# A new hand-written order of all operations in a gated recurrence with a highway layer

## The chip, the cores and the metric

The kernel runs on one core of one Trainium2 chip. The metric is the device time of one execution in microseconds (us). The kernel before took 206.16 us (median of three runs, 205.93 to 207.3).

A core has five engines that work side by side, each through its own queue in order: TensorE (PE; its weight loads are listed as PEld), VectorE (DVE), ScalarE (ACT), GpSimd (POOL), and SyncE (SP), which here only issues transfers. Engines wait for each other by semaphores. TensorE writes to PSUM; GpSimd works on SBUF alone.

## The reference

A recurrence along the sequence with a forget gate, and then a highway layer on each token:

```python
# x, f_logit: (4, 6336, 256) float32; lower_bound: (256,)
sig = 1.0 / (1.0 + np.exp(-f_logit))
f = lower_bound + (1.0 - lower_bound) * sig
h = 0
for t in range(S):
    h = f[:, t] * h + (1.0 - f[:, t]) * x[:, t]
    y[:, t] = h
# on y as (25344, 256), with w_h, w_t (256, 256) and b_t (256,)
H = np.maximum(y @ w_h, 0.0)
T = 1.0 / (1.0 + np.exp(-(y @ w_t + b_t)))
out = T * H + (1.0 - T) * y
```

## The kernel before

The 25344 tokens are cut into 29 units of 2, 4 or 8 blocks of 128 tokens (`parts`: units 0 and 1 have 2 blocks, 2 to 4 have 4, 5 to 26 have 8, 27 has 4, 28 has 2). Features lie in two halves of 128, numbered 0 and 1. Each unit goes through the same steps. A step is a token in a long string, `order`: a letter, the unit, a dot, the half (or piece), and after a colon the number of the buffer it takes. A trailing `v` puts a step on VectorE that otherwise goes to ScalarE (f, c) or GpSimd (b, e).

- l, x (line 256, SP): load the logits and x of a unit, 1 MB each for 8 blocks.
- u (268, ScalarE): u = sigmoid(-logits), so that 1 - f = (1 - lower_bound) * u.
- b (276, GpSimd or VectorE): bv = u * x for one half; two inputs in SBUF.
- i (284, TensorE): transposes u into PSUM (uT). f (295 ScalarE, 293 VectorE): f = 1 + ncc * uT, ncc being lower_bound - 1.
- p (304, TensorE): transposes bv into PSUM (bT).
- s (323, VectorE): the scan y = f * y + bT along the tokens; it carries over from unit to unit.
- z, g (335 and, with the weights already loaded, 115; TensorE): the two products of y with the weights.
- t (348, ScalarE): t = sigmoid(z + b_t). d (352, VectorE): d = max(ncc * y, g), that is H - y (y itself is kept without its factor 1 - lower_bound).
- e (358, GpSimd or VectorE): d = d * t, in pieces; two inputs in SBUF. A unit of 8 blocks has both halves in one tile of 2048 columns, cut at 1024 and 1536 into e.0, e.1 and e.2; units 9 to 21 have one piece of 2048. Smaller units have one piece for each half.
- o (380, 381, TensorE): transposes y (times 1 - lower_bound) and d back and adds them in PSUM. c (393 ScalarE, 391 VectorE): copies that to SBUF. w (397, SP): stores it, 512 KB at a time for most units.

Tokens without a number are the set-up: pc and pb transpose lower_bound and b_t, cc computes ncc and cc from lower_bound (lines 200 and 201, VectorE), cb copies the bias, dg scales the identity (217, VectorE), IW and WHa/WTa prepare the weights (212 GpSimd, 228 ScalarE). A k token gives TensorE idle matmuls to do.

The program issues the steps exactly in the order of the string, and each engine keeps that order (`tc.keep_in_program_order`). So the string is each engine's queue, and a step that waits holds up everything behind it on its engine.

One function ties GpSimd to VectorE beyond the data:

```python
def shared(ins, gpsimd):
    if not gpsimd:
        held[:] = [ins]
    elif held:
        tc.add_manual_dep(ins.ins, held.pop().ins.name, ..., reason="shared port")
```

It is called for each b and e, for IW and for dg: a product of GpSimd waits for the last product of VectorE that stands ahead of it in the string. Nothing makes a product of VectorE wait for GpSimd's earlier one.

Of the kernel before, what the change touches and what calls it, by code (L numbers as in the profile page):

```python
# [57 lines left out]
b6.0:5 f6.1:2 d4.0 k*3:1 p6.1:0 s6.1:4 i6.0:1 l8:2 u7:3 z5.1:1 g5.1:2 x8:2 b7.1:6 b7.0:7 f6.0:0 t4.0 t5.1:2 i7.1:1 p6.0:0
z5.0:0 f7.1:1 d5.1:2 t5.0 o3.0:1 g5.0:2 i7.0:1 c3.0:3 s6.0:5 e5.1v w1.0 l9:3 e4.0 x9:3 w0.0 e5.2v p7.1:0 l10:4 w2.0 d5.0 e5.0
g6.0:0 z6.1:1 z6.0:2 u8:0 f7.0:3 t6.1:1 i8.0:1 e4.1v b8.0:1 b8.1:0 s7.1:6 f8.0v:2 l11:5 w3.0 t6.0 x10:4 x11:5 u9:1 d6.0:0  # L60
i8.1:0 g6.1:1 p7.0:1 s7.0:7 o5.1:2 f8.1:0 c5.1:1 o5.0:0 i9.1:0 d6.1 e6.0 p8.1:1 c5.0:0 f9.1:1 e6.2 z7.0:2 t7.0:0 o4.0:0
p8.0:0 c4.0:2 u10:2 w5.1 b9.1:3 e6.1 l12:0 w4.0 l13:1 g7.1:1 s8.1:2 i9.0:1 g7.0:2 o6.0:0 s8.0:3 i10.1:0 f9.0:3 b9.0:2 x12:0
# [375 lines left out]
```

## Time and profile before

| | before |
|---|---|
| time, median of 3 runs | 206.16 us (205.93 to 207.3) |
| profiled execution: span, first to last instruction | 204.7 us; its own time is not given, the median lies 1.46 us above the span |
| busy: TensorE, VectorE, ScalarE, GpSimd | 191.6, 193.0, 193.1, 175.6 us |
| granted TensorE clock | 0.996 |
| DMA | 78.4 MB on one queue, 94.7% of 16 engines' span |

The profile is of one execution. A row of a group gives line, engine, operation, `out<-in`, shapes and count, then the busy time in us and the mean ns of one instruction, then the engine's idle time just before them and what ended it. A row in order of time gives start (us), duration (us), engine, line, operation and, in brackets, the idle time before. A row of a wait gives who waited for whom, the sum in us, how often, and the longest. Consecutive instructions of an engine overlap a little in their records, so a busy time is less than the sum of durations.

### The profile page before, as it was taken

The page shows a single profiled execution, that of the slowest core. Times are in us where ns is not written, and L with a number is a line of the kernel's source. Part 1 is how long each engine was busy: PE and PEld are TensorE (multiplying, and loading weights), DVE is VectorE, ACT ScalarE, POOL GpSimd, SP SyncE. Part 2 cuts the span into 40 slices and gives each one's busy share as a digit, 9 for nine tenths or more (in the row PEclk, how much of TensorE's full clock was granted, in tenths as well). Part 3 has the DMA queues.
Part 4 walks back from the last instruction along what each step waited for, and adds up shares of the span by engine and source line. Part 5 has one row for each costly group of instructions (what it writes and reads, how often), then busy time and mean ns, then how long its engine had stood idle before and what let it go on. Part 6 is the DMA issues. An engine that isn't in the chain of part 4 may idle for free. (4 is left out here: it accounts for less than half of the span.)

```text
span 204.7 us, 4658 instructions
## 1 busy us (share of the span) xinstructions
PE 191.6 (94%) x1826; PEld 131.9 (64%) x1826; DVE 193.0 (94%) x162; ACT 193.1 (94%) x201; POOL 175.6 (86%) x98
## 2 busy tenths in 40 slices
PE   7889999989899899999999999999998999999990
PEld 2455656576567757757666577776776677677680
DVE  2799999999999999999999999999999999999990
ACT  4799999999999999999999999999999999999771
POOL 3146699899996999799999979999979999989960
PEclk9999999999999999999999999999999999999998
DMA  5999999999999999999999999999999998970986
GB/s 176 387 415 429 410 421 415 413 424 420 422 419 411 429 423 415 425 415 422 428 402 426 429 417 419 418 425 423 413 337 400 425 390 307 352 283 22 396 330 241
DMA packets 16413, 78.68 MB, mean 384 GB/s; under 512 B 1796, under 2 KB 2568, under 8 KB 10760
## 3 DMA queue, kind: packets, MB, share of 16 engines
q1 hardware_dynamic: 16384, 78.39, 94.7%
q8 instruction: 14, 0.23, 0.4%
q14 instruction: 7, 0.06, 0.1%
q10 hardware_dynamic: 8, 0.00, 0.0%
HBM read 52.43 MB, written 25.95 MB: 383 GB/s over the span
## 5 line engine op out<-in xcount | busy, mean ns | idle before, releaser
L276 POOL TENSOR_TENSOR bv<-u,x 128x1024 bf16<-128x1024 f16 (+2 forms) x53 | 104.2, 1988 | 14.8 <-DVE d L358 5.7
L323 DVE TENSOR_TENSOR_SCAN y<-f,y,bT 128x1024 bf16<-128x1024 f16 (+5 forms) x56 | 106.9, 1925 | 0.2
L358 POOL TENSOR_TENSOR d<-d,t 128x512 bf16<-128x512 bf16 (+3 forms) x32 | 70.4, 2213 | 4.1 <-DVE d L358 1.8
L352 DVE SCALAR_TENSOR_TENSOR d<-y,ncc,g 128x1024 bf16<-128x1024 bf16 (+2 forms) x58 | 63.2, 1105 | 0.3 <-PE g L115 0.2
L348 ACT ACTIVATE t<-z,bt 128x1024 bf16<-128x1024 f32 (+2 forms) x58 | 62.4, 1112 | 0.8 <-PE z L115 0.8
L295 ACT ACTIVATE f<-uT,ncc 128x1024 f16<-128x1024 f16 (+2 forms) x55 | 60.8, 1120 | 0.8 <-DVE y L323 0.2
L393 ACT COPY o<-op 128x1024 f32<-128x1024 f32 (+2 forms) x53 | 52.8, 1036 | 1.9 <-ACT t L348 1.0
L268 ACT ACTIVATE u<-l 128x2048 f16<-128x2048 f32 (+2 forms) x29 | 51.5, 1776 | 2.5 <-DMA l<-in_f_logit_dram 2.5
L380 PE MATMUL op<-diag,y 128*128 128x128 f16 x396 | 49.7, 219 | 0.9 <-ACT t L348 0.4
L381 PE MATMUL op<-ident_b,d 128*128 128x128 bf16 x396 | 49.7, 219 | 0.8 <-POOL d L358 0.8
L381 PEld LDWEIGHTS <-d 128*128 128x128 bf16 x396 | 44.0, 113 | 4.8 <-POOL d L358 1.7
L380 PEld LDWEIGHTS <-y 128*128 128x128 bf16 x396 | 44.2, 113 | 2.3
L335 PE MATMUL z<-y,w_sb 128*128 128x512 bf16 (+1 forms) x116 | 40.0, 368 | 0.8 <-DVE d L352 0.3
L335 PE MATMUL g<-y,w_sb 128*128 128x512 bf16 (+1 forms) x116 | 40.3, 368 | 0.0
L304 PE MATMUL bT<-ident_f,bv 128*128 128x128 f32 x198 | 32.1, 278 | 2.9 <-DVE y L323 1.1
L115 PE MATMUL g<-y,w_sb 128*128 128x512 bf16 x88 | 33.3, 379 | 0.0
L115 PE MATMUL z<-y,w_sb 128*128 128x512 bf16 x88 | 33.3, 379 | 0.0
L284 PE MATMUL uT<-ident_h,u 128*128 128x128 f16 x396 | 31.4, 219 | 2.0 <-DVE y L323 1.1
L284 PEld LDWEIGHTS <-u 128*128 128x128 f16 x396 | 25.9, 98 | 11.1 <-issue 3.1
L335 PEld LDWEIGHTS <-w_sb 128*128 128x128 f16 x232 | 22.3, 98 | 15.7 <-ACT f L295 0.2
L304 PEld LDWEIGHTS bT<-ident_f,bv 128*128 128x128 f32 x198 | 22.1, 140 | 13.3 <-issue 4.7
L115 PEld LDWEIGHTS <-w_sb 128*128 128x128 f16 x176 | 17.2, 98 | 15.8 <-issue 1.7
(35 smaller groups left out, 53.6 us busy)
## 6 DMA issues: line engine op xcount, KB each, us to landing
out_dram<-o SPq DMA_DIRECT2D x48, 512.0 KB, 9.7
l<-in_f_logit_dram SPq DMA_DIRECT2D x22, 1024.0 KB, 14.0
x<-in_x_dram SPq DMA_DIRECT2D x22, 1024.0 KB, 14.3
l<-in_f_logit_dram SPq DMA_DIRECT2D x4, 512.0 KB, 6.3
x<-in_x_dram SPq DMA_DIRECT2D x4, 512.0 KB, 7.6
x<-in_x_dram SPq DMA_DIRECT2D x3, 256.0 KB, 3.7
l<-in_f_logit_dram SPq DMA_DIRECT2D x3, 256.0 KB, 4.3
out_dram<-o SPq DMA_DIRECT2D x2, 256.0 KB, 14.8
```

What stands on the lines that cost most here:

```text
L115: return pe.add_instruction(mybir.InstMatmult(name=nc.get_next_instruction_name(), start_tensor_calc=start, stop_tensor_calc=stop, tile_si ...
L276: shared(pin(e.tensor_mul(bv[:, :nb // 2].rearrange("p k d j -> p k j d"), st[n]["u"][:, :nb, own].rearrange("p (k j) d -> p k j d", j=2), ...
L284: pin(nc.tensor.transpose(uT[:, j * P:(j + 1) * P], st[n]["u"][:, j, h * P:(h + 1) * P], ident_h))
L295: pin(nc.scalar.activation(to, of, AF.Identity, scale=ncc[:, h:h + 1], bias=1.0))
L304: pin(nc.tensor.transpose(words[:, k:k + g * (P - 1) + 1:g], pair, ident_f))
L323: pin(nc.vector.tensor_tensor_scan(y[:, c:e], st[n]["f", h][:, c:e], st[n]["bT", h][:, c:e], 0.0 if fresh else carry[h], op0=ALU.mult, op1 ...
L335: pin(nc.tensor.matmul(p[:, a:e], w, half(n, "y", ki)[:, a:e], start=ki == 0, stop=ki == NH - 1))
L348: pin(nc.scalar.activation(half(n, "t", m), st[n]["z", m][:, :tokens(n)], AF.Sigmoid, bias=bt[:, m:m + 1]))
L352: pin(nc.vector.scalar_tensor_tensor(half(n, "d", m), half(n, "y", m), ncc[:, m:m + 1], st[n]["g", m][:, :tokens(n)], op0=ALU.mult, op1=AL ...
L358: shared(pin(e.tensor_mul(st[n]["d"][:, a:c], st[n]["d"][:, a:c], st[n]["t"][:, a:c])), not eng)
L380: pin(nc.tensor.matmul(o, half(n, "y", h)[:, cols], diag[:, h], start=True, stop=False))
L381: pin(nc.tensor.matmul(o, half(n, "d", h)[:, cols], ident_b, start=False, stop=True))
```

## The change

Only the string changes. It has 850 tokens in both versions, and they name the same computation; their places, some buffers, and some of the trailing `v` differ:

- f on VectorE: units 1.0, 8.0, 10.0; now also 28.0.
- e on VectorE: before 0.0, 0.1, 1.0, 1.1, 2.0, 2.1, 3.1, 4.1, 5.1, 5.2, 7.1, 7.2, 8.1, 11.0, 15.0, 16.0, 19.0, 23.0, 23.2, 24.2, 26.1, 26.2 (22 pieces). After: 0.0, 0.1, 1.0, 1.1, 4.1, 6.1, 7.1, 8.2, 11.0, 15.0, 16.0, 19.0, 23.0, 23.2, 25.0, 25.1, 26.2, 27.1, 28.0, 28.1 (20 pieces). The others are GpSimd's.
- c on VectorE: before 11.0, 26.1, 26.2, 27.1; after 1.0, 11.0, 26.0.
- The five b on VectorE stay (0.0, 0.1, 1.0, 1.1, 2.1).
- Buffers for o: numbers 0 to 3 for nearly all units before, 0 to 4 after.

The beginning, the places around e15, e16 and e19, and the end, of the diff:

```diff
-k*3:a0 x0:0 pc:0 l0:0 l1:1 cc u0:0 k*3:1 pb:2 i0.0:1 k*4:0 dg wh u1:1 b0.1v:0 f0.0:0 b0.0v:1 i1.0:0 x1:1 l2:2 wt IW f1.0v:1 p0.0:1
-WHa cb i0.1:0 s0.0:0 f0.1:2 x2:2 b1.1v:2 b1.0v:3 k*2:0 i1.1:1 k*1:0 p0.1:0 f1.1:3 p1.0:1 s0.1:1 k*1:0 p1.1:0 l3:3 g0.0:0
-s1.0:2 g0.1:1 u2:2 s1.1:3 x3:3 k*1:2 i2.1:1 d0.1:0 l4:4 WTa d0.0 g1.0:2 i2.0:0 g1.1:1 z1.1:0 b2.1v:4 f2.1:0 d1.1:1 d1.0
...
-c14.0:0 f19.1:2 z17.1:1 p18.0:0 e16.0v c14.1:1 b19.1:6 w14.0 b19.0:7 x21:3 e15.0v i19.0:1 t17.1:2 g17.0:2 z17.0:0 f19.0:3
...
-e28.1 w26.1 c27.1v:3 o28.0:2 c27.0 o28.1:a1 w26.0 c28.0:2 c28.1:4 w27.0 w28.0 w28.1
+x0:0 k*1:0 l0:0 k*3:a0 u0:0 i0.0:1 pc:1 cc i0.1:0 b0.0v:0 k*3:2 f0.1:0 l1:1 f0.0:1 p0.0:0 wh u1:1 pb:0 b0.1v:1 p0.1:1 k*4:1 s0.0:0 x1:1
+s0.1:1 IW i1.1:0 f1.1:2 i1.0:1 l2:2 WHa b1.1v:2 k*2:2 b1.0v:3 p1.1:0 wt f1.0v:3 x2:2 p1.0:1 cb u2:2 g0.0:1 k*3:2 g0.1:0 s1.1:2 s1.0:3
+dg l3:3 i2.1:0 WTa f2.1:1 x3:3 i2.0:1 z1.0:2 d0.1:0 b2.1v:4 z0.0:0 l4:4 p2.1:0 f2.0:0 t1.0:0 d0.0 u3:3 s2.1:4 z1.1:1 b2.0:5 t0.0:1
...
+s17.1:1 o14.0:2 f18.1:2 w11.1 t16.0:2 t16.1 i19.0:0 x20:2 f19.0:1 o14.1:0 b19.0:5 b18.0:4 z17.0:1 c14.1:0 c14.0:1 t17.0:0 e16.0v e15.0v
+b18.1:1 p18.0:1 i19.1:0 o16.1:0 b20.1:0 g17.0:2 c16.1:2 f19.1:0 s18.0:4 o16.0:1 p18.1:1 z17.1:0 w13.0 d17.0:1 c16.0:4 g17.1:2 s18.1:5
...
+w23.0 b28.1:6 o25.0:0 z26.1:1 o25.1:a1 c25.0:0 g26.1:0 d26.0:1 s27.0:3 e25.2 e26.0 t26.1 o25.2:2 o25.3:1 d26.1 c25.1 p28.0:0 w24.1
+c25.2:4 e26.2v c25.3 s28.0:6 g27.0:a1 z27.0:2 t27.0:2 o26.3:0 w24.0 w22.1 c26.3:1 e26.1 d27.0:2 z27.1:1 w20.1 t27.1 p28.1:0 o26.2:2
+g27.1:a1 o26.1:0 o26.0:1 c26.2 s28.1:7 e27.0 z28.0:a0 d27.1 w25.0 z28.1:a1 g28.1:2 e27.1v w25.1 c26.1:3 t28.0:1 o27.0:0 c26.0v o27.1:a0
+g28.0:1 d28.1:0 t28.1 e28.1v d28.0 c27.0:2 e28.0v o28.0:2 c27.1 o28.1:0 w26.1 c28.0:0 w26.0 w27.0 w28.0 c28.1:4 w28.1
```

More of the change, by code (lines that the diff above doesn't have):

```diff
@@ L58 @@
[L58 to L62, printed above, removed]
@@ new lines @@
+o21.1:1 g23.1:2 f28.1:0 e22.0 i28.0:0 b25.0:2 o22.0:0 c21.1:3 f28.0v:1 u26:0 d23.1 g24.1:1 p25.0:1 s25.0:0 i25.1:0 z24.1:2 c22.0:1
+x26:2 x27:3 e22.2 b25.1:3 w21.1 l27:4 z24.0:0 f25.1:3 b26.1:1 t24.1:2 i26.1:0 x28:4 w22.0 d24.1:2 p25.1:1 z23.0:2 t24.0 w20.0 f26.1:2
+e24.2 b26.0:4 g24.0:1 s25.1:1 t23.0 o22.1:0 u27:3 p26.1:0 z25.1:2 c22.1:3 d24.0 e24.0 e23.1 b27.0:5 e24.1 w21.0 i26.0:1 b27.1:7 e23.2v
+e23.0v t25.1:1 f26.0:3 g25.0:1 o23.1:0 z25.0:2 p26.0:1 s26.1:4 c23.1:1 i27.1:0 d25.0:0 o23.0:0 w23.1 s26.0:5 t25.0 o24.1:1 f27.1:2
```

71 lines of the change are left out of this document (32 added, 39 removed).

## The prediction

> **What bounds the kernel now.** I read the page's busy shares first, then the engines' busy time by stage, then the groups of instructions with their shapes, then the waits, and last the order of time at the start, at the end and around VectorE's products. The page:
>
> ```profile
> span 204.7 us, 4658 instructions
> PE 191.6 (94%) x1826; PEld 131.9 (64%) x1826; DVE 193.0 (94%) x162; ACT 193.1 (94%) x201; POOL 175.6 (86%) x98
> ```
>
> Three engines at 94% say little, because the share mixes the ramp, the middle and the tail. So I cut the span where GpSimd's first bv begins (12.37), where its first e begins (26.70), where its last bv begins (189.06) and where its last e ends (199.62):
>
> ```profile
> core 0: us, PE busy (x) PEld busy (x) DVE busy (x) ACT busy (x) POOL busy (x), PEclk, DMA share, GB/s
> 0.00:12.37 12.37, 10.31 (x50) 4.39 (x50) 6.87 (x19) 8.09 (x15) 2.49 (x13) 1.00 0.82 305
> 12.37:26.70 14.33, 13.34 (x113) 8.45 (x113) 14.09 (x20) 14.12 (x20) 10.01 (x7) 1.00 1.02 421
> 26.70:189.06 162.36, 157.18 (x1545) 111.18 (x1546) 162.13 (x111) 161.98 (x153) 154.45 (x71) 1.00 0.97 393
> 189.06:199.62 10.56, 10.31 (x115) 7.64 (x112) 9.92 (x14) 7.96 (x14) 8.63 (x9) 1.00 0.91 358
> 199.62:204.70 5.08, 0.45 (x5) 0.28 (x5) 0.00 (x0) 0.90 (x3) 0.00 (x1) 0.83 0.63 241
> ```
>
> In the middle VectorE (DVE) idles 0.23 of 162.36 us and ScalarE (ACT) 0.38. No reordering can squeeze those two there; only less work on them can. GpSimd (POOL) idles 7.91 there, and in the tail 10.56 - 8.63 = 1.93, together 9.84. ScalarE has room in the tail, 10.56 - 7.96 = 2.60, and in the first stage. The waits say what the idle time is:
>
> ```profile
> POOL bv L276 <- DVE d L358: 5.7, 5, 1.4
> DVE ncc L200 <- PE lbT L194: 3.0, 1, 3.0
> ACT u L268 <- DMA l<-in_f_logit_dram: 2.5, 2, 1.3
> DVE f L293 <- PE uT L284: 1.4, 1, 1.4
> ```
>
> GpSimd's largest wait is for VectorE's e (the manual dependency in `shared`). ScalarE waited for loads only at the start, though the DMA engines are 97% busy in the middle: loads arrive in time, without much to spare.
>
> **The change, part by part.** The terms come from these groups (busy us, mean ns):
>
> ```profile
> L358 DVE TENSOR_TENSOR d<-d,t 128x2048 bf16<-128x2048 bf16 x4 | 5.3, 1354 | 0.0
> L358 DVE TENSOR_TENSOR d<-d,t 128x1024 bf16<-128x1024 bf16 x1 | 0.7, 678 | 0.0
> L358 DVE TENSOR_TENSOR d<-d,t 128x512 bf16<-128x512 bf16 x13 | 5.1, 424 | 0.1
> L358 DVE TENSOR_TENSOR d<-d,t 128x256 bf16<-128x256 bf16 x4 | 0.9, 282 | 0.0
> L391 DVE COPY o<-op 128x512 f32<-128x512 f32 x3 | 2.1, 691 | 0.4 <-PE op L381 0.2
> L293 DVE TENSOR_SCALAR f<-uT,ncc 128x256 f16<-128x256 f16 x1 | 0.5, 483 | 1.4 <-PE uT L284 1.4
> L295 ACT ACTIVATE f<-uT,ncc 128x256 f16<-128x256 f16 x5 | 2.4, 491 | 0.0
> L393 ACT COPY o<-op 128x512 f32<-128x512 f32 x9 | 5.1, 588 | 1.8 <-ACT t L348 1.0 <-PE op L381 0.8
> L358 POOL TENSOR_TENSOR d<-d,t 128x1024 bf16<-128x1024 bf16 x8 | 17.5, 2189 | 2.0 <-ACT t L348 1.0 <-DVE d L358 0.6 <-DVE d L352 0.3
> L358 POOL TENSOR_TENSOR d<-d,t 128x512 bf16<-128x512 bf16 x13 | 15.0, 1168 | 1.7 <-DVE d L358 1.2 <-PE uT L284 0.5
> L358 POOL TENSOR_TENSOR d<-d,t 128x256 bf16<-128x256 bf16 x2 | 1.4, 682 | 0.4 <-ACT t L348 0.4
> L276 POOL TENSOR_TENSOR bv<-u,x 128x1024 bf16<-128x1024 f16 x44 | 94.8, 2178 | 8.5 <-DVE d L358 5.7 <-ACT u L268 2.1 <-issue 0.4
> ```
>
> *Which engine does what.* Counting the tokens of both orders by size: VectorE's e goes from 4, 13, 1 and 4 pieces (256, 512, 1024, 2048 columns) to 6, 8, 2 and 4; its f gains f28.0 (256); its copies lose one of 512. That is -5 x 0.424 + 0.678 + 2 x 0.282 + 0.483 - 0.691 = -1.09 us. Two records fewer also overlap their neighbours less, so I count -1.0. ScalarE gains a copy and loses an f: 0.588 - 0.491 = +0.10. GpSimd takes five more pieces of 512 and gives up one of 1024 and two of 256: 5 x 1.168 - 2.189 - 2 x 0.682 = +2.29. TensorE's matmuls, the idle ones included (27 in both), and the bytes moved are the same.
>
> The GPSIMD Engine Reference of the Trainium skill (its opening part) calls GpSimd the wrong place for ordinary elementwise work, because VectorE is roughly twice as fast. The rows above differ in size: 1168 against 424 ns is 2.8 times. By the page's factor the same moves would add about 0.8 us to GpSimd, an estimate; I use the rows.
>
> *The run-ins.* Two groups of before show a cost:
>
> ```profile
> 85.81 1.20 DVE L358 TENSOR_TENSOR d<-d,t 128x2048 bf16<-128x2048 bf16 x1
> 149.09 1.78 DVE L358 TENSOR_TENSOR d<-d,t 128x2048 bf16<-128x2048 bf16 x1
> 147.61 2.19 POOL L276 TENSOR_TENSOR bv<-u,x 128x1024 bf16<-128x1024 f16 x1
> 120.43 2.35 DVE L358 TENSOR_TENSOR d<-d,t 128x2048 bf16<-128x2048 bf16 x2
> 121.78 3.01 POOL L276 TENSOR_TENSOR bv<-u,x 128x1024 bf16<-128x1024 f16 x1 [1.44 <-DVE d L358]
> 61.73 0.53 DVE L358 TENSOR_TENSOR d<-d,t 128x512 bf16<-128x512 bf16 x1
> ```
>
> The e at 149.09 (e19.0) starts while GpSimd's bv of 147.61 runs until 149.80, and takes 1.78 instead of 1.20: +0.58 on VectorE. e8.1 at 61.73 takes 0.53, 0.11 over its group's mean. The other way round, b19.1 starts at 121.78, 0.2 us into VectorE's second large e (e15.0), and takes 3.01 instead of 2.18: +0.83 on GpSimd, nothing on VectorE. If no run-in is left, VectorE saves 0.58 + 0.11 = 0.69 and GpSimd 0.83; if as many come back elsewhere, zero. In the new order e16.0 and e15.0 stand together ahead of b18.1, so GpSimd waits out both, 2.35 us: what the run-in cost it returns as a wait. I take the whole 0.69 for VectorE and nothing for GpSimd's waits. Two operations new on VectorE can hold up its queue, c1.0 (ahead of d3.1) and f28.0 (ahead of d23.1), if op or uT is not there: between nothing and the 0.24 that the copy at 198.85 (below) waits for its op; I count nothing.
>
> VectorE's sum: -1.0 - 0.69 = **-1.7 us**.
>
> *Start.*
>
> ```profile
> 3.86 0.26 PE L194 MATMUL lbT<-ident_f,lb 2*128 2x2 f32 x1
> 4.14 0.63 ACT L268 ACTIVATE u<-l 128x512 f16<-128x512 f32 x1 [1.29 <-DMA l<-in_f_logit_dram]
> 4.16 0.16 DVE L200 TENSOR_SCALAR ncc<-lbT 128x2 f32<-128x2 f32 x1 [3.03 <-PE lbT L194]
> 5.96 0.63 ACT L268 ACTIVATE u<-l 128x512 f16<-128x512 f32 x1 [1.19 <-DMA l<-in_f_logit_dram]
> 7.44 0.68 DVE L323 TENSOR_TENSOR_SCAN y<-f,bT 128x256 bf16<-128x256 f16 x1
> ```
>
> TensorE now does i0.0 ahead of lbT. i0.0 needs u0, which ends at 4.14 + 0.63 = 4.77; so lbT moves from 3.86 to about 5.1 and VectorE's ncc/cc from 4.16 to about 5.4, 1.2 later. Queued behind cc on VectorE are both b0 pieces, then s0. In exchange f1.0, whose wait for uT of unit 1 cost 1.4 us (the waits above), no longer stands in front of s0.0: it comes after both s0 and both b1, when u1 (done at 6.6) is long turned. So 1.4 of idle time goes and 1.2 comes; the scan s0.0 moves from 7.44 to about 6.8, and what VectorE has done by the end of s1 is the same set. ScalarE now waits for cc from 4.77 to about 5.8 (1.0) where it waited 1.19 for l1; u1 stands behind f0.1 and f0.0 and starts near 6.5 instead of 5.96, but those two are done earlier. I credit it with 0.2. I count the start as 0, with 0.4 either way. SP's first 20 loads keep their order but for x8, which now waits behind the first store, while l9 goes ahead of it; the queue was full there (share 1.02 in the second stage), so x8's bytes change places with l9's. I count nothing; if x8 comes late for b8, the wait is at most one load's spacing, 2.5 us at 421 GB/s for 1 MB, of which waiting pieces of e cover a part. Later stores stand further back on SP (w0.0 behind l10 and l12; w20.1 and w22.1 behind w24.0), with five o buffers in use all along instead of four. So loads come a little earlier in the middle. From w24.1 on there are nine stores of 512 KB as before, and the DMA share there is 0.91: nothing, or one store's 1.5 us at 358 GB/s if they queue up.
>
> *Tail.*
>
> ```profile
> 195.61 2.93 POOL L358 TENSOR_TENSOR d<-d,t 128x512 bf16<-128x512 bf16 x3 [1.19 <-DVE d L358]
> 198.13 0.48 DVE L352 SCALAR_TENSOR_TENSOR d<-y,ncc,g 128x256 bf16<-128x256 bf16 x1
> 198.85 0.69 DVE L391 COPY o<-op 128x512 f32<-128x512 f32 x1 [0.24 <-PE op L381]
> 198.95 0.67 POOL L358 TENSOR_TENSOR d<-d,t 128x256 bf16<-128x256 bf16 x1 [0.41 <-ACT t L348]
> 199.28 1.35 ACT L393 COPY o<-op 128x512 f32<-128x512 f32 x3 [0.41 <-ACT t L348]
> ```
>
> Now the last product is GpSimd's e28.1, ending at 199.62; two small ScalarE copies end at 200.63, and the store and the end of the program take 4.07 more. In the new order VectorE does the last products (e27.1, e28.1, e28.0: 0.424 + 2 x 0.282), and GpSimd's last is e27.0. Behind VectorE's end lies the same o, copy and store, so the end follows VectorE's end as it does now.
>
> *What the other two allow.* VectorE alone would give -1.7. ScalarE has no less work (+0.10), so it must idle less: it can give about 0.2 at the start and perhaps half of its tail's 2.60, its copies there waiting for products: -1.5 at best, and I take -1.0. GpSimd behind 26.70: VectorE's products that it must wait out add up to 4 x 1.20 + 7 x 0.424 + 2 x 0.678 = 9.1 (units 4, 6, 7, 8, 11, 15, 16, 19, 23, 25, 26; the last three lie behind GpSimd's end); its extra work is 2.29 - 0.83 = 1.5, of which one piece of 1.17 (e2.1) goes into the second stage, where it idles 4.3. It also starts about 0.4 earlier: b2.1 on VectorE has one d of 256 columns (0.48) less ahead of it, and GpSimd's first bv waits for b2.1. So it needs 9.1 + 1.5 - 1.2 - 0.4 = 9.0 of the 9.84 it idles now: room for a gain of 0.8. The smallest of 1.7, 1.0 and 0.8 sets the end: **-0.8 us**. The profiled span goes from 204.7 to 203.9. The median of 206.16 lies 1.46 above the profiled span; the same added gives **205.4 us**.
>
> **The rivals.** *All of VectorE's gain is kept.* The new order closes ScalarE's tail gaps by 1.7 and GpSimd's waits overlap with its own lack of data. For it: VectorE sets the pace for 162 us. Against: ScalarE's 0.38 idle in the middle. With the 0.24 that VectorE waits at 198.85 gone too and the start 0.2 better (1.4 against 1.2): -2.1, 204.0 us.
>
> *GpSimd becomes the bound (slower).* Each hand-over costs more than the product itself: at 121.78 GpSimd idled 1.44 around a product of 1.20, so 0.2 for each of nine groups, +1.9. Then it needs 9.0 + 1.9 = 10.9 of 9.84, ends 1.1 late, bT and the scans behind it too; and behind its last piece now lie o27, d28.0 and e28.0 (four blocks of matmuls, one d and one e, about 1.6) which before lay beside it: +2.7, 208.9 us. It decides if GpSimd's last piece ends after about 198.0. The page SBUF — State Buffer of the Trainium skill (section Who interferes with whom) says that the two share a port pair as an exclusive lock, so that whichever comes second is blocked outright. The two large run-ins above agree (0.58 and 0.83 lost). By that rule every VectorE product is GpSimd's lost time whatever the order, which is this rival without the hand-overs.
>
> *The change doesn't do what it says.* Only GpSimd waits for VectorE's earlier product; nothing makes a VectorE product wait for GpSimd's. If the pace differs from the planned one, run-ins come back elsewhere (0.58 or 0.83 each) and gaps open on the full engines: VectorE's 0.69 is lost, and a wait as long as the 0.24 above comes in place of the 0.2 won at the start: the rest, 0.8 less 0.9, is no gain, 206.2 us.
>
> **How the numbers follow.** Forecast 0.47, all of the gain 0.20, no gain 0.20, GpSimd's bound 0.13. About 1% (2.06 us) is what a measurement of this kernel can tell from no change: faster means under 204.1, slower over 208.2. Over half of the second case and some of the first lie under 204.1: 0.17. Most of the last and a little of the third lie over 208.2: 0.12. The rest, 0.71, is between. The range leaves out the far side of the two outer cases: 203.7 to 207.9.
>
> **What would show it.** In the changed profile: VectorE's busy time near 191.3 with 160 records; no e of 2048 columns over 1.25 and no bv over 2.3 us; ncc near 5.4 and s0.0 near 6.8; GpSimd's busy time near 177, its waits for VectorE's e still the largest; ScalarE's idle time in the tail down by about a us. The forecast falls if VectorE idles more than 1 us between the ramp and the last scan, above all in bT or y waits behind GpSimd's bv, or if GpSimd's last piece ends after 198.0.

## The result: 4% slower, and the profile after

The changed kernel takes 216.72 us (median of four runs, 213.96 to 218.68), where the kernel before took 206.24 us beside it. The ratio is 1.041, with an interval of 1.035 to 1.047; ratios here and below leave the disturbed, longest executions out, so they can differ from the quotient of the medians. The forecast was 205.4 us with a range of 203.7 to 207.9, so both failed. The profiled execution took 213.96 us and is the shortest of the four; its span is 212.2 us, 7.5 more than before.

The changed string has fewer lines, so e is line 354 here (358 before), d 348, the scan 319, bv 272, t 344, lbT 190; in e6, e9 and e10 e is line 357, in the other experiments 358. The page of the changed kernel:

```profile
span 212.2 us, 4617 instructions
PE 190.8 (90%) x1799; PEld 132.7 (63%) x1826; DVE 200.3 (94%) x160; ACT 194.1 (91%) x201; POOL 178.3 (84%) x100
```

VectorE has two records fewer and is busy 7.3 us longer. By stage, cut as before about where GpSimd's first bv begins, at 26.70, where its last bv begins and where its last e ends (the first e now comes at 20.2, so 26.70 is kept only for comparison):

```profile
core 0: us, PE busy (x) PEld busy (x) DVE busy (x) ACT busy (x) POOL busy (x), PEclk, DMA share, GB/s
0.00:12.20 12.20, 9.65 (x49) 4.18 (x50) 6.63 (x18) 7.28 (x14) 2.68 (x14) 1.00 0.86 307
12.20:26.70 14.50, 12.00 (x97) 7.83 (x99) 13.86 (x18) 14.19 (x21) 12.16 (x10) 1.00 1.03 422
26.70:197.20 170.50, 158.64 (x1538) 112.67 (x1561) 169.50 (x112) 163.26 (x152) 157.26 (x74) 0.99 0.95 377
197.20:205.00 7.80, 7.75 (x84) 5.73 (x83) 7.67 (x9) 6.33 (x11) 6.15 (x5) 1.00 0.88 345
205.00:212.20 7.20, 2.71 (x38) 2.25 (x36) 2.70 (x7) 3.06 (x7) 0.09 (x1) 1.00 0.68 260
```

In the middle ScalarE now idles 170.50 - 163.26 = 7.24 us, where it idled 0.38. VectorE still looks full (1.00 idle). One of the two limits has become longer, and the other waits for it. The groups show which instructions grew:

```profile
L354 DVE TENSOR_TENSOR d<-d,t 128x512 bf16<-128x512 bf16 x8 | 7.2, 922 | 0.2
L354 DVE TENSOR_TENSOR d<-d,t 128x2048 bf16<-128x2048 bf16 x4 | 7.1, 1802 | 0.0
L354 DVE TENSOR_TENSOR d<-d,t 128x1024 bf16<-128x1024 bf16 x2 | 3.3, 1638 | 0.0
L354 POOL TENSOR_TENSOR d<-d,t 128x512 bf16<-128x512 bf16 x18 | 21.5, 1206 | 1.0 <-DVE d L354 0.8 <-DVE d L348 0.2
```

The same products took 424, 1200 (undisturbed) and 678 ns before. The excess (the time beyond the undisturbed duration) is 8 x (922 - 424) + 4 x (1802 - 1200) + 2 x (1638 - 678) = 8.3 us, against 0.69 before. So these fourteen records hold 7.6 us more, about as much as the span has grown (7.5). In order of time, VectorE's and then GpSimd's rows around three of the places:

```profile
42.68 2.86 DVE L354 TENSOR_TENSOR d<-d,t 128x512 bf16<-128x512 bf16 x2
93.92 2.75 DVE L354 TENSOR_TENSOR d<-d,t 128x2048 bf16<-128x2048 bf16 x1
186.19 3.14 DVE L354 TENSOR_TENSOR d<-d,t 128x512 bf16<-128x512 bf16 x2
```

```profile
41.81 2.16 POOL L272 TENSOR_TENSOR bv<-u,x 128x1024 bf16<-128x1024 f16 x1
43.92 2.64 POOL L354 TENSOR_TENSOR d<-d,t 128x512 bf16<-128x512 bf16 x2
93.45 5.23 POOL L272 TENSOR_TENSOR bv<-u,x 128x1024 bf16<-128x1024 f16 x2
184.37 2.16 POOL L272 TENSOR_TENSOR bv<-u,x 128x1024 bf16<-128x1024 f16 x1
186.50 2.29 POOL L354 TENSOR_TENSOR d<-d,t 128x1024 bf16<-128x1024 bf16 x1
```

The e at 93.92 (e11.0) begins 0.47 us into b16.1, which runs to 95.60, and ends at 96.67, 1.07 us behind that piece: it waited for it and then did its work. Such a wait doesn't appear as idle time; it is inside the record of the instruction that waits. Two products stand in the rows at 42.68 (e4.1 and e6.1: 1.57 and 1.37 instead of 0.42 each) and at 186.19 (e23.2, and behind it e23.0 of 1024 columns, which runs on to 189.34). In full: e4.1 met b8.1 (+1.14), e6.1 e4.0 (+0.95), e8.2 b11.0 (+1.73), e11.0 b16.1 (+1.53), e19.0 b22.0 (+0.85), e23.2 b26.0 (+0.19), e23.0 e24.0 (+1.92). In each case GpSimd was 1 to 9 us behind its place in the string when VectorE came: the piece ahead of e11.0 in the string, b15.1, ended at 102.9, nine after VectorE had reached e11.0.

The waits of the changed kernel, and three rows of its start:

```profile
POOL bv L272 <- DVE d L354: 8.8, 4, 3.1
ACT t L344 <- PE z L111: 4.9, 5, 2.0
DVE ncc L196 <- PE lbT L190: 4.7, 1, 4.7
POOL bv L272 <- DMA x<-in_x_dram: 3.2, 2, 2.3
```

```profile
5.33 0.28 PE L280 MATMUL uT<-ident_h,u 128*128 128x128 f16 x2 [0.98 <-ACT u L264]
5.80 0.16 DVE L196 TENSOR_SCALAR ncc<-lbT 128x2 f32<-128x2 f32 x1 [4.67 <-PE lbT L190]
7.03 0.69 DVE L319 TENSOR_TENSOR_SCAN y<-f,bT 128x256 bf16<-128x256 f16 x1
```

ScalarE's t now waits for z, that is, for scans that come late. ncc starts at 5.80 (4.16 before), but the 1.4 us wait of f1.0 is gone. VectorE reaches its first e, with the same steps behind it, at 15.87 instead of 15.34: 0.5 us later, 0.4 of it idle time and the rest longer records.

A run-in also stops TensorE here. The scan behind e4.1 and e6.1 came 2.1 us late, TensorE stood for it, and then its granted clock read 0.50 for 3.4 us (rows of TensorE, and that stretch of the stages):

```profile
47.85 0.61 PE L280 MATMUL uT<-ident_h,u 128*128 128x128 f16 x8 [2.02 <-DVE y L319]
49.24 0.63 PE L111 MATMUL g<-y,w_sb 128*128 128x512 bf16 x1
48.60:52.00 3.40, 3.40 (x14) 1.54 (x13) 3.40 (x3) 1.40 (x3) 3.40 (x3) 0.50 1.01 422
```

Matmuls of 512 columns began 0.43 us apart there, and 0.22 apart outside it. The longest of ScalarE's waits for z (2.0 us, up to 51.68) and a wait of VectorE's scan for bT (0.84 us, up to 53.24) lie in or just behind this stretch. In e2, e12 and e15 the same pause of 2.0 us came without it.

### The profile page after: what moved, and what is told of

Read it like the earlier page. It is cut to its first block, busy times and chain, and to the rows that moved or that the text cites. A ratio compares the mean times of both kernels' runs of the same rounds, so it can differ in the third digit from the quotient of the medians.

```text
span 212.2 us, 4617 instructions
## 1 busy us (share of the span) xinstructions
PE 190.8 (90%) x1799; PEld 132.7 (63%) x1826; DVE 200.3 (94%) x160; ACT 194.1 (91%) x201; POOL 178.3 (84%) x100
## 4 chain that ended last, share of the span: by engine, by line
DVE 19%; PE 12%; issue 11%; POOL 11%; DMA 9%; ACT 6%; SPq 1%; ACTq 0%; DVEq 0%; POOLq 0%
DVE y L319 9%; POOL bv L272 7%; DVE d L348 6%; DMA x<-in_x_dram 5%; DMA out_dram<-o 4%; POOL d L354 4%; ACT o L389 3%; PE op L377 3%; DVE d L354 2%; PE op L376 2%; PE g L331 2%; PE z L331 2%; ACT t L344 2%; ACT f L291 1%; PE bT L300 1%
## 5 line engine op out<-in xcount | busy, mean ns | idle before, releaser
L354 POOL TENSOR_TENSOR d<-d,t 128x512 bf16<-128x512 bf16 (+2 forms) x34 | 73.2, 2164 | 4.3 <-DVE d L348 2.3
L344 ACT ACTIVATE t<-z,bt 128x1024 bf16<-128x1024 f32 (+2 forms) x58 | 57.7, 1020 | 5.7 <-PE z L111 4.9
L291 ACT ACTIVATE f<-uT,ncc 128x1024 f16<-128x1024 f16 (+2 forms) x54 | 55.2, 1034 | 2.6 <-PE uT L280 1.4
L389 ACT COPY o<-op 128x1024 f32<-128x1024 f32 (+2 forms) x54 | 49.4, 944 | 3.6 <-PE op L377 1.7
L376 PE MATMUL op<-diag,y 128*128 128x128 f16 x396 | 50.4, 220 | 0.5 <-DVE d L348 0.4
L264 ACT ACTIVATE u<-l 128x2048 f16<-128x2048 f32 (+2 forms) x29 | 49.0, 1689 | 1.8 <-DMA l<-in_f_logit_dram 1.8
L331 PE MATMUL z<-y,w_sb 128*128 128x512 bf16 (+1 forms) x115 | 40.5, 372 | 2.2 <-DVE d L348 1.6
L111 PE MATMUL z<-y,w_sb 128*128 128x512 bf16 x80 | 30.8, 385 | 0.0
L111 PE MATMUL g<-y,w_sb 128*128 128x512 bf16 x74 | 28.4, 384 | 0.0
```

The costliest lines, as they stand in the source:

```text
L111: return pe.add_instruction(mybir.InstMatmult(name=nc.get_next_instruction_name(), start_tensor_calc=start, stop_tensor_calc=stop, tile_si ...
L291: pin(nc.scalar.activation(to, of, AF.Identity, scale=ncc[:, h:h + 1], bias=1.0))
L331: pin(nc.tensor.matmul(p[:, a:e], w, half(n, "y", ki)[:, a:e], start=ki == 0, stop=ki == NH - 1))
L344: pin(nc.scalar.activation(half(n, "t", m), st[n]["z", m][:, :tokens(n)], AF.Sigmoid, bias=bt[:, m:m + 1]))
L354: shared(pin(e.tensor_mul(st[n]["d"][:, a:c], st[n]["d"][:, a:c], st[n]["t"][:, a:c])), not eng)
L376: pin(nc.tensor.matmul(o, half(n, "y", h)[:, cols], diag[:, h], start=True, stop=False))
```

## The experiments

**The met products, and the others.** The theory after the result: the loss is VectorE's e's that begin while GpSimd runs. The first pair leaves out either those that met a piece or seven that met none; e3 removes the order's only protection from the kernel before. A product left out makes those blocks of the output wrong and takes its own work away too.

```diff
 e1
-p8.1:0 e4.1v c5.0:4 e6.1v c5.1:1 ... e8.2v e7.1v ... e11.0v ... e19.0v ... e23.2v e23.0v
+p8.1:0 c5.0:4 c5.1:1 ... e7.1v
 e2
-... e7.1v ... e16.0v e15.0v ... e25.0v e25.1v ... e26.2v ... e27.1v
+... (all seven left out)
```

> The new order with seven of VectorE's e left out (4.1, 6.1, 8.2, 11.0, 19.0, 23.2, 23.0: those that in the new order's trace started while a piece of GpSimd's ran); their columns of d stay without their factor t, so this part of the result is not computed. Left out work that has the duration it has when nothing is in its way: 4 x 0.34 + 2 x 1.14 + 0.60 = 4.2 us. Theory (these seven wait on VectorE's own queue for GpSimd's piece to end, 8.4 us in all, and VectorE sets the time): the time falls by more than their own 4.2 us, from 215 to 203 to 206 us, where ScalarE's full queue stops it; VectorE's busy time falls by 11 to 13 us. Rival (the new order is slow for other reasons, its start, late GpSimd products, loads): it falls by no more than 4.2 us, to 210 to 212 us.

Measured: 217.49 us (1.051, 1.048 to 1.054), no faster than the changed kernel. The theory's number is missed, and the trace shows how:

```profile
60.63 1.26 DVE L352 SCALAR_TENSOR_TENSOR d<-y,ncc,g 128x1024 bf16<-128x1024 bf16 x1
61.81 9.20 DVE L358 TENSOR_TENSOR d<-d,t 128x512 bf16<-128x512 bf16 x1
70.93 1.27 DVE L352 SCALAR_TENSOR_TENSOR d<-y,ncc,g 128x1024 bf16<-128x1024 bf16 x1
```

```profile
60.08 2.15 POOL L358 TENSOR_TENSOR d<-d,t 128x1024 bf16<-128x1024 bf16 x1
68.55 2.17 POOL L276 TENSOR_TENSOR bv<-u,x 128x1024 bf16<-128x1024 f16 x1
71.08 2.14 POOL L276 TENSOR_TENSOR bv<-u,x 128x1024 bf16<-128x1024 f16 x1 [0.36 <-DVE d L358]
```

e7.1, which met nothing in the changed kernel, came during e7.0 and waited out six pieces, passed over at five of their ends, up to 70.73, where b12.0, held for e7.1 itself, made GpSimd stop. One product of 0.42 us took 9.20. Meanwhile TensorE stood for 7.8 us (64.41 to 72.25), its granted clock read 0.51 from 67.4 to 77.6, and ScalarE waited up to 9.6 us for z. So this time doesn't tell what the seven met products cost.

> The new order with seven other e of VectorE left out (7.1, 15.0, 16.0, 25.0, 25.1, 26.2, 27.1), those that met nothing; their columns of d stay without t. Their own duration is the same: 4 x 0.34 + 2 x 1.14 + 0.60 = 4.2 us. Theory: only the own work goes, the seven that meet GpSimd still wait: 210 to 213 us, 5 us or more above the kernel without the seven that met. Rival (other reasons): the two kernels lie within 1.5 us of each other.

Measured: 214.56 us (1.038, 1.035 to 1.040). The seven run-ins stayed where they were, 7.8 us of excess, and the 4.2 us of work left out hardly shortened the time: VectorE now waits 4.1 us for bT where it waited 0.8. Neither the theory's numbers nor the rival's are met, and the pair doesn't separate the cost of the met products, because leaving products out changes who meets whom and who waits.

```diff
 e3, in shared()
-        elif held:
+        elif held and False:
```

> The kernel before, with the extra dependency taken away (no GpSimd product waits for VectorE's; it is no data dependency). Theory: VectorE's products now meet running pieces of GpSimd and wait for their end, a piece's half on average (0.6 to 1 us for a 1024 piece, more for 2048) at some ten places: VectorE's busy time grows by 5 to 10 us and the time from 206 to 210 to 215 us. Rival (the hold costs more, GpSimd's 7.5 us of waits for VectorE are what the time hangs on): no change or faster, 203 to 206 us.

Measured: 222.59 us median (217.95 to 225.82), more than the theory's 210 to 215. In the profiled execution, the longest of the four, seven products meet a piece for long, 18.4 us of excess in all, the worst of them e16.0:

```profile
126.81 9.21 DVE L358 TENSOR_TENSOR d<-d,t 128x2048 bf16<-128x2048 bf16 x2
```

(e16.0 with e15.0 behind it; e16.0 alone took 8.08 and waited out four pieces.) So the kernel before is fast because its products nearly always come at the end of a piece, and the hold keeps the next piece off. Its own four meetings (e5.1, e8.1, e19.0, e23.2) lie 0.02 to 0.70 us ahead of a piece's end.

**One run-in, priced.** Only e11.0's hold is removed from the kernel before:

```diff
-        shared(pin(e.tensor_mul(...)), not eng)
+        ins = pin(e.tensor_mul(...))
+        if n != 11:
+            shared(ins, not eng)
```

> The kernel before with one hold taken away: GpSimd's b14.0 no longer waits for VectorE's e11.0 (no data dependency). In the trace of before b13.0 ends at 85.66 and e11.0 starts at 85.81, so b14.0 will run when e11.0 arrives. Theory (a VectorE product that meets a GpSimd piece waits for its end, and every us of that is a us of the time): e11.0 takes 3 us or more instead of 1.2 and the time goes from 206.2 to 208 or more; if it loses at several piece ends in a row, more. Rival (such a wait is taken up by slack behind it): within 0.5 us of before, 205.8 to 206.8.

Measured: 208.56 us (208.29 to 216.15; 1.010, 1.007 to 1.013). VectorE's and GpSimd's rows:

```profile
86.01 3.03 DVE L358 TENSOR_TENSOR d<-d,t 128x2048 bf16<-128x2048 bf16 x1
```

```profile
85.78 5.26 POOL L276 TENSOR_TENSOR bv<-u,x 128x1024 bf16<-128x1024 f16 x2
```

e11.0 lost 1.83 us, the span grew by 1.8 (206.5) and the time by about 2: this run-in cost its full length. b14.1 behind it lost 1.0, and nothing beyond e11.0's 1.83 shows in the span.

**The start, first attempt.**

```diff
-x0:0 k*1:0 l0:0 k*3:a0 u0:0 i0.0:1 pc:1 cc i0.1:0
+x0:0 k*1:0 l0:0 k*3:a0 u0:0 pc:1 i0.0:1 cc i0.1:0
```

> The new order with one token moved: pc (the transpose of lower_bound that VectorE's first work waits for) back ahead of i0.0. Theory: the start costs VectorE 1.6 us at its first instruction and gives 1.4 back at f1.0, so the time falls by at most 1.5 us, to 213 to 215 us, and run-ins of the same kind stay, on the same or other pieces. Rival (the late start shifts VectorE against GpSimd, and that shift makes the run-ins): they go with it, 205 to 208 us.

Measured: 217.41 us (1.044, 1.036 to 1.051), span 212.7: no gain, where the theory had 213 to 215. The same run-ins, 8.8 us of excess. ncc started at 4.59, and s0.0 then waited 1.41 us: what I had counted as an even exchange at the start was one.

**Early products back on VectorE.** A rival explanation was that GpSimd is late because the new order gives it e2.1, e2.0 and e3.1 early on.

```diff
-... e2.1 ... e2.0 ... e3.1
+... e2.1v ... e2.0v ... e3.1v
```

> The new order with e2.1, e2.0 and e3.1 back on VectorE, as before the change (GpSimd -3.4 us, VectorE +1.0 us, all early). In the new order's trace GpSimd runs without a gap from 18 to 64 us and is 6 to 9 us behind its places in the string when e4.1, e6.1, e8.2 and e11.0 come. Theory A (these pieces put GpSimd behind): the run-ins of units 4 to 11 (5.4 us) mostly go, those of 19 and 23 stay: 208 to 212 us. Rival B (GpSimd's lag comes from elsewhere and 3.4 us do not close it): as many run-ins, on the same or other pieces: 213 to 218 us.

Measured: 219.07 us (1.060, 1.058 to 1.063). VectorE falls back as far as GpSimd gains, two more products meet pieces, and the excess is 9.6 us. Theory A falls; the time is even above the 213 to 218 us of rival B.

**Moving the met products, or leaving all out.** In e5 the seven go to places where the piece ahead has ended when VectorE comes (the lines below are the first and the last of the moves); in e6 all sixteen products behind the ramp are left out, so no run-in is possible.

```diff
 e5
-i8.1:0 t6.1 e4.0 e6.2 ... p8.1:0 e4.1v c5.0:4 e6.1v c5.1:1
+i8.1:0 t6.1 e4.1v e6.1v e4.0 e6.2 ... p8.1:0 c5.0:4 c5.1:1
 ...
-e24.0 e23.1 b27.0:5 e24.1 w21.0 i26.0:1 b27.1:7 e23.2v e23.0v
+e23.2v e23.0v e24.0 e23.1 b27.0:5 e24.1 w21.0 i26.0:1 b27.1:7
```

> The new order with the seven products that met GpSimd moved a few places, everything still computed: e4.1 and e6.1 ahead of e4.0, e11.0 ahead of b16.1, e23.2 and e23.0 ahead of e24.0 (so that GpSimd holds that piece back until VectorE's product is done), e19.0 behind d20.1, and e8.2 and e7.1 behind d9.0 and f10.0 and ahead of e8.0. VectorE's order changes only at e19.0 and e8.2. Theory (the time is VectorE's own work plus the run-ins): from the trace of the new order 1.3 (e4.1's wait for b8.1) and 0.3 (e23.2's) stay and 6.8 of 8.4 us go; since later pieces shift, up to 3 us may come back: 207 to 211 us, VectorE's busy time 193 to 196. Rival (GpSimd's time is what counts; holding it back costs as much as it saves): 213 to 216 us.

Measured: 212.67 us (1.026, 1.022 to 1.030), VectorE busy 195.0. Three run-ins were left (e4.1 +1.1, e8.2 +1.1, e23.2 +0.2). It is faster than the changed kernel, but above the 207 to 211 us that the removed run-ins were to give.

> The new order without any e on VectorE behind the ramp (sixteen pieces left out: 4.1, 6.1, 7.1, 8.2, 11.0, 15.0, 16.0, 19.0, 23.0, 23.2, 25.0, 25.1, 26.2, 27.1, 28.0, 28.1; their columns of d stay without t). No run-in is possible after 18 us and no hold either. Their own duration is 9.2 us, their waits in the new order's trace 8.4. Theory: the time falls from 215 to 201 to 205 us, where ScalarE's 193 us of work and its start and tail stand. Rival (the new order has another fault of several us beside the run-ins): 207 us or more.

Measured: 209.28 us (1.013, 1.011 to 1.015). The rival holds: with no run-in and VectorE busy for only 184.8 us, 15.5 less than in the changed kernel, it is still slower than before, so the new order has a second fault.

**The start, second attempt.** In e6 TensorE paused 0.42 us for u0, and then began its idle matmuls of 512 columns 0.43 us apart up to 10.1 us; the next, from 11.2 us on, came 0.22 apart. In the kernel before they came 0.22 apart from 5.5 us on, behind no pause. TensorE's rows of e6, and below them those of e9, where the pause is filled:

```profile
8.01 1.49 PE L114 MATMUL idle<-zeros 128*128 128x512 bf16 x3
```

```profile
7.67 0.81 PE L114 MATMUL idle<-zeros 128*128 128x512 bf16 x3
```

```diff
-x0:0 k*1:0 l0:0 k*3:a0 u0:0 i0.0:1 pc:1 cc i0.1:0
+x0:0 k*1:0 l0:0 k*3:a0 pc:1 cc k*2:2 u0:0 i0.0:1 i0.1:0
```

> The sixteen VectorE products e behind the ramp are left out, as in e6_no_vector_e, and the start is mended: pc and cc stand ahead of u0 and i0.0 again, and two idle matmuls more fill TensorE's pause there. Theory (TensorE's pause at 4.8 us keeps its matmuls at half speed up to about 10 us, and VectorE pays): the first idle matmul at full speed comes before 8 us instead of 11.2, VectorE's idle time up to the scan s4.1 falls from 7.7 to 6.7 us or less, and the time goes from 209.28 to 207.7 to 208.7. Rival (what the start loses is hidden by later waits): 209.0 to 209.6.

Measured: 207.37 us, equal to before (1.002, 1.000 to 1.005), with VectorE's idle time up to s4.1 down from 7.6 to 6.6 us and ScalarE's f1.1 waiting 1.3 us for uT instead of 2.7. The mended start is worth 1.9 us there. The edit both fills the pause and moves the transpose of lower_bound forward, and no run parts the two. A pause alone doesn't decide when full speed comes: e4 paused 0.46 us and has it from 7.3 us, the changed kernel's profiled execution paused 0.98 and has it from 5.8, and in other traces of the same start it was 9.4 to 11.2. The Trainium skill (TensorE: Matmul & The Clock Gate, Part 1: The HAM clock gate) says that TensorE starts at half rate and speeds up behind a window of about 3.4 us of activity that runs freely. The pairs of rows agree on the factor of two, and the spread of 5.8 to 11.2 us would go with a free window; the length of the window was not measured at the start.

> The new order with only the start mended. Theory (the start costs about 1.9 us in most executions, the run-ins stay): 213 to 215.5, excess of the products 7 to 9 us. Rival (the mended start shifts VectorE against GpSimd and the run-ins change with it): excess under 6 or over 10, the time outside 213 to 215.5.

Measured: 214.93 us (1.041, 1.036 to 1.045), excess 10.3 us, since e7.1 now meets b11.0 as well (+1.9). The time lies where the theory put it, 1.8 below the changed kernel's median, but the ratios of the two are alike, and the rival's shift of VectorE against GpSimd is there too. What the start costs the whole kernel isn't settled; it is nothing in the profiled execution.

**Loads ahead of stores.** In e6 and e9 SP stands at stores that wait for copies, up to 10 us at a time, and some loads behind them (l17, l19, x18 and others) land within 0.2 us of their use. 28 loads were moved ahead of such stores:

```diff
-w5.0 w3.0 ... w2.0 ... l13:1 ... x12:0
+l13:1 x12:0 w5.0 w3.0 ... w2.0
 ...
-... w11.0 l19:1 x19:0 w9.0 l20:2 ... x18:1 ... w12.1
+... l19:1 x19:0 l20:2 x18:1 w11.0 w9.0 ... w12.1
```

> As e9_none_start_mended, and 28 loads from l13 on stand ahead of the store at which SP stood and waited before issuing them (ahead of w5.0, w6.0, w8.0, w10.1, w11.0, w12.1 and so on). Theory (in the new order loads land just when they are needed or late because SP waits at stores ahead of them): GpSimd's waits for x (7.6 us in e6_no_vector_e) and ScalarE's for l (3.3) fall to under 4 us together and the time lies 1 to 2.5 us under that of e9_none_start_mended, at 205.5 to 207.5. Rival (the DMA engines are full, an earlier load only makes a store later): the waits for loads go, waits for output buffers or for stores take their place, and the time is within 0.7 us of e9_none_start_mended.

Measured: 214.68 us (1.038, 1.035 to 1.041), 7 us slower than e9. The theory falls, and not as the rival had it: the cost is far from nil. The waits of e10:

```profile
POOL d L357 <- DVE d L351: 10.4, 6, 5.3
DVE d L351 <- PE g L114: 6.9, 4, 5.3
ACT o L392 <- DMA out_dram<-o: 6.7, 3, 3.6
PE g L334 <- ACT o L392: 4.3, 3, 3.8
```

Read from the third line: copies wait for an output buffer whose store has not been done, g waits for the copies' PSUM, d for g, GpSimd's e for d; and TensorE, which stood for 3.8 us there (60.3 to 64.1), had a granted clock of 0.51 from 62.2 to 69.0. w5.0 landed at 62.9 instead of 56.9. The DMA engines are full up to there (e9 moves 383 to 426 GB/s in the slices up to 70 us, but for the first), so each load that goes first makes a store late, and the stores were the more urgent.

> The whole new order with nothing left out, the seven products of e5_moved_where_met at their other places, the start mended and the 28 loads earlier. Theory (three faults that add up: run-ins, start, loads): against e5_moved_where_met (212.67) it loses 1 for the start and 1 to 2.5 for the loads, and run-ins of about 2.5 us are left: 208 to 211. Rival (only the run-ins count): 212 to 213.

Measured: 218.23 us (1.054, 1.050 to 1.058); the loads spoil it in the same way (ScalarE waits 7.3 us for stores).

> The new order with its products where they are, the start mended and the 28 loads earlier. Theory (the run-ins do not come from late loads): VectorE's e of 2048 columns still take over 2 us in units 11, 19 and 23, e8.2 and e4.1 over 1 us, an excess of 7 to 9 us in all, and the time is 211 to 214.5. Rival (GpSimd meets VectorE's products because its bv were kept waiting for loads): the excess falls under 4 us and the time lies under 210.

Measured: 216.52 us (1.046, 1.042 to 1.049), 8.3 us of excess, though e19.0 met nothing here; the time is 2 us above what the theory gave, since the loads cost here too. Run-ins do not come from late loads.

**The new order repaired, with nothing left out.** The start of e9, the moves of e5, and two more:

```diff
-t6.0:1 b8.1:0 i8.0:0 f8.0v:3 ... i8.1:0 t6.1 e4.0 e6.2 ... p8.1:0 e4.1v c5.0:4 e6.1v
+t6.0:1 i8.0:0 f8.0v:3 ... i8.1:0 t6.1 e4.0 e4.1v e6.1v b8.1:0 e6.2 ... p8.1:0 c5.0:4
 ...
-t8.0 e8.0 b11.1:7 x12:0 e8.2v e7.1v b12.0:0 w4.0 w5.1 d9.0:0 f10.0v:1 ... s10.1:4
+t8.0 d9.0:0 f10.0v:1 s10.1:4 e8.2v e7.1v e8.0 b11.1:7 x12:0 b12.0:0 w4.0 w5.1
```

> The new order with nothing left out: the start mended as in e9_none_start_mended, the seven products moved as in e5_moved_where_met, and the three that still met a piece there moved on: b8.1 behind e4.0, e4.1 and e6.1 ahead of it; s10.1, e8.2 and e7.1 ahead of e8.0. Theory (run-ins and start are the loss): 212.67 - 1.9 (start) - 1.15 - 1.1 (two run-ins) gives 207.5 to 209.5, with an excess of the products under 1 us. Rival (a further fault comes with products on VectorE): over 210.5 although the excess is under 1 us.

Measured: 211.32 us (1.021, 1.017 to 1.025). e4.1 and e8.2 meet next to nothing now (+0.15, 0), but e11.0, which e5 had freed, meets b14.0 (+1.36); the excess is 1.7 us. The rest is in VectorE's waits between 20 and 200 us, 0.4 us in the kernel before:

```profile
DVE y L323 <- PE bT L304: 1.5, 3, 0.8
DVE d L352 <- POOL bv L276: 1.1, 1, 1.1
DVE d L352 <- PE g L115: 0.9, 2, 0.5
DVE y L323 <- issue: 0.6, 1, 0.6
DVE d L358 <- ACT t L348: 0.3, 1, 0.3
```

Against the kernel before, 1.0 more of run-ins, 4.0 more of these waits, 0.6 at the start, 0.5 of smaller gaps, and 0.9 less behind VectorE's last instruction (4.2 instead of 5.2 us) make 5.2 us; the span is 5.3 longer (210.0). So mending the meetings by hand buys waits: a product put ahead of a piece holds that piece, and bv and bT come late. The rival's number is right; its condition, excess under 1 us, was not met.

**The rule of a meeting.** A train of 44 GpSimd pieces of 1024 columns behind the kernel before, and beside it 26 VectorE products at many phases:

```diff
+    for k in range(44):
+        pin(nc.gpsimd.tensor_mul(gp["d"][:, :1024], gp["d"][:, :1024], gp["t"][:, :1024]))
+    for k in range(26):
+        for _ in range(1 + k % 3):
+            filler(512 - 32 * (k % 5))
+        n = (512, 512, 2048, 512)[k % 4]
+        pin(nc.vector.tensor_mul(ve["d"][:, :n], ve["d"][:, :n], ve["t"][:, :n]))
```

> The kernel before, and behind its last step a train of its own: 44 pieces of 1024 columns on GpSimd, one behind the other (2.19 us each), and beside it on VectorE 26 products of 512 or 2048 columns, each behind one to three operations that read PSUM, so that they begin at many points of a piece. Theory A (whoever waits gets in at the next boundary): no product of 512 takes more than 2.19 + 0.42 = 2.6 us, none of 2048 more than 3.4, and the next piece of GpSimd takes longer by about what VectorE's product has left. Theory B (GpSimd's next piece can go ahead of a product that waits): some products take the length of several pieces, 4.4 us and more, as e7.1 did with 9.2 us in e1_without_met; then their share is what the run is for.

Measured, the groups of the train (GpSimd's, VectorE's), and one meeting on VectorE:

```profile
L419 POOL TENSOR_TENSOR d<-d,t 128x1024 bf16<-128x1024 bf16 x44 | 99.9, 2271 | 3.4
L429 DVE TENSOR_TENSOR d<-d,t 128x512 bf16<-128x512 bf16 x20 | 25.6, 1280 | 0.0
L429 DVE TENSOR_TENSOR d<-d,t 128x2048 bf16<-128x2048 bf16 x6 | 11.2, 1858 | 0.0
```

```profile
258.02 2.31 DVE L429 TENSOR_TENSOR d<-d,t 128x512 bf16<-128x512 bf16 x1
```

The longest of 512 took 2.31 us, the longest of 2048 2.58: theory A for all 26. The 21 products that came more than 0.15 us ahead of the running piece's end lost that remainder less 0.12 to 0.15 (the one at 258.02 had 2.03 to wait and lost 1.88); the other five lost nothing. The fillers, which read PSUM, waited for nothing. GpSimd's next piece mostly took 2.18 behind a product of 512 and 2.98 behind one of 2048, against 2.12 with nothing beside it. Outside the train, 71 of 75 meetings with 0.14 us or more to wait followed the same rule. Three waited out several pieces (e7.1 in e1, e16.0 and e23.2 in e3: six, four and two) and got in only where GpSimd had no next piece ready to run. One, e26.1 in e3, lost nothing with 1.45 us left: that piece had itself begun during e26.2, just ahead. What lets GpSimd's next piece go first isn't seen in any trace and stays open.

**VectorE alone lighter, in the kernel before.** e7.2 now stands behind o7.1, which reads it, so four blocks of unit 7 lack that factor; the instructions are all there.

```diff
-e8.1v e7.2v t9.1 e7.1v ... b11.1:7 t8.0
+e8.1v t9.1 e7.1v ... b11.1:7 e7.2 t8.0
 ...
-d20.1:1 f22.0:1 e19.0v l24:0 ... d20.0 p22.0:0
+d20.1:1 f22.0:1 l24:0 ... d20.0 e19.0v p22.0:0
```

> The kernel before with two steps moved: e7.2 (512 columns) is GpSimd's, behind b11.1, and e19.0 stands behind d20.0, where GpSimd's b23.1 has ended. VectorE has 0.42 us less work and the 0.58 us run-in at 149.09 goes: 1.0 us in all, in the stretch where VectorE idles 0.23 and ScalarE 0.38 us. Theory (as in the prediction: the smallest of what the three engines allow sets the end, and ScalarE has no less work): VectorE idles 1 us more and the time stays within 0.5 us of before. Rival (VectorE sets the pace alone): 0.8 to 1.2 us faster, 205.7 to 206.2.

Measured: 207.97 us (1.007, 1.005 to 1.009): slower than either theory has it. VectorE's rows, and GpSimd's wait:

```profile
61.28 1.18 DVE L358 TENSOR_TENSOR d<-d,t 128x512 bf16<-128x512 bf16 x2
85.46 1.72 DVE L358 TENSOR_TENSOR d<-d,t 128x2048 bf16<-128x2048 bf16 x1
```

```profile
POOL bv L276 <- DVE d L358: 7.4, 6, 2.7
```

e19.0 now takes its 1.22, but b23.0 is held 2.7 us, d20.0 waits 0.8 us for its g, and d21.1 0.6 behind GpSimd's bv: the move cost more in waits than the 0.58 it saved. e8.1 (0.84 instead of 0.53) and e11.0 (1.72 instead of 1.20) meet longer remainders. At e8.1 this isn't the edit's doing: nothing ahead of it was changed, and this execution was 0.45 us earlier at e0.1 already (14.89 instead of 15.34). At e11.0 VectorE came 0.35 us earlier and b13.0, with e7.2 now on GpSimd ahead of it, ended 0.44 later. So meetings change with an edit and also from one execution to the next. No version made here beats the kernel before.

## Why the prediction was wrong, point by point

**What bounds.** Right, and it helps in reading the result: VectorE and ScalarE were both full, so time added to VectorE alone shows in the span and as idle time of ScalarE (in e8 1.83 us added made the span 1.8 longer).

**VectorE's own work, -1.0.** Mostly right: e, f and copies without run-ins were 14.6 - 0.7 = 13.9 us in the groups before and are 21.4 - 8.3 = 13.1 after, 0.8 less. In the whole busy time, 192.3 against 192.0 without run-ins, 0.3 of it is left; b0.1, next to GpSimd's IW, took 0.3 longer, and some scans a little.

**The run-ins, -0.69.** This is the step that failed. I wrote "if no run-in is left, VectorE saves 0.58 + 0.11 = 0.69 ...; if as many come back elsewhere, zero", and so took zero as the worst. They went from 0.69 to 8.3: +7.6 instead of -0.69, a miss of 8.3 us, as large as the distance between -0.8 forecast and +7.5 measured for the span. The match holds for the profiled execution. It doesn't mean that the order without run-ins would be as fast as forecast: e14, with 1.7 us of them left, takes 211.32 us, since waits came in their place. Two things were wrong in it. The price: I took the two sizes that the trace happened to show, 0.58 and 0.83, where a meeting costs what is left of GpSimd's piece less 0.14, up to 2.0 us for a piece of 1024 columns, and in e1 8.8 us. And the number: it was bounded by what the kernel before had, and that kernel had so few only because its products come at or near a piece's end. I had the fact that decides it in hand (only GpSimd waits for VectorE), and did not ask, product by product, where GpSimd would be when VectorE came.

**The rival that the change doesn't do what it says.** It named the mechanism, gave it 0.20 and priced it at no gain, 206.2. The mechanism is shown by e3, e5 and e8; its price was too low by all of the 7.5 us. This also makes the forecast of the range wrong: its upper end came from GpSimd's hand-overs.

**The slower rival, GpSimd as the bound.** It fell. GpSimd's last piece does end late (205.1, where 198.0 was the limit I gave), but with 178.3 us busy of 212.2 it followed VectorE. Its waits for VectorE's e, 8.8 + 0.8 us, are close to the 9.1 that I summed. Two small sums there were off, and neither enters the 205.4 us: twice VectorE's 0.88 us is 1.8, not the 0.8 given as an estimate for GpSimd's added work, and nine hand-overs of 0.24 are 2.2, not 1.9. The Trainium skill (SBUF — State Buffer, Who interferes with whom) has the pair as an exclusive lock where the second comer is fully blocked; I weighed it only as GpSimd's lost time. The rows agree with it, and it holds for VectorE too: e13 shows the block for each of the 21 products that came more than 0.15 us ahead of a piece's end. e1 and e3 show besides that a blocked product can be passed over by several pieces.

**Start, 0 with 0.4 either way.** ncc at 5.80 and s0.0 at 7.03, where I had 5.4 and 6.8, because l0 was late and u0 ended at 5.28 instead of 4.77. In the profiled execution VectorE came 0.5 us later to its first e, just outside the bound: 0.4 of idle time, and longer records, b0.1's beside IW above all, which the sum had not. What I missed is TensorE's pause: e9 against e6 prices the mended start, the pause and the place of lower_bound's transpose together, at 1.9 us in that order, and in the whole kernel it is not settled.

**Transfers, 0.** Loads did come later in the middle, not earlier as I had it: GpSimd waited 3.2 us for x. e10 to e12 show that this is no fault of SP's order that earlier loads could mend. f28.0 and c1.0 on VectorE cost nothing that the groups show.

**What I said would show it.** The e of 2048 columns took up to 2.75 (limit 1.25), bv up to 3.13 (limit 2.3), VectorE was busy 200.3 us (191.3): the signs that I had named did tell. GpSimd's busy time, 178.3, was right within 1.3.

## What to carry to other kernels

Where two engines exclude each other and only one of them is made to wait, an order is safe only for the pace it was made for: take from the trace, for each product, how far the other engine is behind its place in the order at that moment, and price a meeting by the longest piece it can fall into. A wait of this kind hides in the busy time, so look for groups whose mean exceeds the undisturbed duration. An edit that moves or removes products on one of the two engines changes the later meetings and waits, and can cost more than it saves (e1, e7, e16).

## What the runs showed of the hardware

- A VectorE product of two bf16 inputs in SBUF that begins during a GpSimd product loses the remainder of that piece less 0.12 to 0.15 us (71 of 75 meetings in the kernels, and all 21 in the train that had more than 0.15 us to wait). The train's operations that read PSUM didn't wait: equal sizes took the same time within 0.015 us.
- Three products waited out two, four and six pieces, until GpSimd had no next piece ready; the longest, a product of 0.42 us, took 9.20.
- GpSimd's piece that begins beside a product of 2048 columns takes 2.98 to 3.14 us instead of 2.12 to 2.18; beside one of 512 in the train, 0.06 longer, and up to 0.26 where the product began just ahead of it.
- Idle matmuls of 512 columns began 0.43 us apart up to 10.1 us in e6 (a pause of 0.42 us at 4.4 us) and 0.22 apart from 7.5 us in e9 (the pause filled). The granted clock read 1.00 in both. A pause of 0.46 us in e4 and of 0.98 in the changed kernel was followed by 0.22 already from 7.3 and 5.8 us.
- During or just behind pauses of TensorE of 2.0, 3.8 and 7.8 us (the changed kernel, e10, e1) its granted clock read 0.50 or 0.51 for 3.4, 6.8 and 10.2 us. In e2, e12 and e15 a pause of 2.0 us was followed by no such stretch.
- Moving 28 loads ahead of stores on one full queue cost 7 us; copies then waited 6.7 us for stores of their output buffers (e10).
